# Sums of a pair two back, similarities at the head of a pair, and a different order of the vector work in the experts

## The chip, the cores and the metric

The kernel runs on one core of a Trainium2 chip. The metric is the device time of one execution in microseconds; the kernel before was run three times and took 657.41, 657.68 and 657.73 us (median 657.68). The engines are named as in the profile: PE (TensorE, matmuls), PEld (its weight loads), DVE (VectorE), ACT (ScalarE), POOL (GpSimd) and SP (SyncE, which issues most DMAs). Each engine runs its own instructions strictly in the order of the program, and engines wait for one another by semaphores.

## The reference, cut to what matters

```python
q, k, v: (4, 8, 768, 64)     # batch, head, sequence, head size
centroids: (8, 16, 64);  w_gate: (512, 8);  w1: (8, 512, 1024);  w2: (8, 1024, 512)

q_assign = argmax(normed(q) . normed(centroids));  k_assign likewise
mask = q_assign[:, :, :, None] == k_assign[:, :, None, :]
scores = where(mask, q @ k.T / 8, -1e9)
attn = softmax(scores) @ v                      # (4, 8, 768, 64)
x = attn as rows (3072, 512)                    # heads side by side
logits = x @ w_gate;  e = argmax(logits);  g = softmax(logits)[e]
out = g * (relu(x @ w1[e]) @ w2[e])             # each row by its own expert
```

Attention is masked to keys of the same cluster as the query. Then each of the 3072 rows goes through the one expert that its gate chooses, with no row dropped.

## The kernel before, in words

**Attention.** Two heads of one batch form a pair; there are NPAIR = 16 pairs, HP = 4 to a batch of B = 4. Pair n runs two loops on PE: twelve `score(n, h, j)` (two halves h of the queries, six blocks j of the keys), and then twelve `attend(n, h, j)`. A score is a float32 product of keys and queries (L433 with qT, kT) and a bfloat16 product of two one-hot masks (L433 with mq, mk) that adds a large number for keys of the same cluster and takes one away for others. ACT makes the exponentials of a score (L445, tile A). DVE adds them up over j (`add_up`, L451, tile acc) for the denominators. `attend` multiplies them with v (L457), and ACT copies the result to oT (L464).

Three kinds of work for other pairs are spread among the scores:

- `sum_up(m)` on PE (L480): column sums of acc, and oT times the gate's weights, into one PSUM bank. `weights_of(m)` on DVE turns that bank (L489), makes the reciprocal denominators and adds to the batch's gate logits. `rows(m)` (DVE, L510) transposes oT, and `store(m)` issues four DMAs (L517) to the rows in memory.
- `prepare(m, step)` makes the masks of a later pair. Step 0 transposes queries and keys on DVE (`turn`, L277). Step 1 is `similar` on PE (L291, four products with the centroids). Steps 2 and 3 are the cluster choice on DVE (`assign0`, `assign1`, `assign2`, L302 to L327, ending with the one-hot transpose ohT). Steps 4 and 5 are `place`: eight ACT instructions (L340 for mk, L337 for mq).
- The gating of a batch, after its last pair: `gate`, `gate_exp`, `gate_sum`, `choose` (L546 to L586), `count` (two small PE products, L592 and L593) and `number` (six DVE instructions and six scatters by POOL, L598 to L607). `count` writes to the upper half of the bank that `sum_up` last took (`BANK`).

The order is written out by hand. `at_pair(n, u, f, ...)` hangs a call behind the score of place u = 6h + j of pair n, u = 12 is after the first half's attends, and 13 after the second's. Several calls at one place run in the order in which they were hung. `load(n + 2)` is issued by SP at the head of pair n. PSUM has three double banks for scores (`ps_s`) and two single banks (`ps_m`) that `similar`, `sum_up`, each half's attend output and some counts take in turn; a taker waits until the one two before it is read out. acc has three buffers, oT two, x one, q_in and k_in two each.

**Experts.** Rows are dealt to ten turns s = 0 to 9 of fixed sizes T: two early ones of 288 rows, then 256, 288, 288, 384, 416, 416, 448 and 128. A turn fetches its expert's weights (SP, 2 MB each), gathers its rows (POOL), weighs and rewrites them (`weigh`, DVE L755), takes them back transposed (`take`, SP; `turn_rows`, DVE L780) and runs two layers on PE. Both layers use a Strassen form: seven products of half matrices where eight would be due, with sums of inputs by DVE (`x_sums`, `w1_sums`, `w2_sums`, `h_sums`, all L789) and sums of outputs (L927). A product of `layer1` or `layer2` is a group of eight matmuls (L969, L1070); leftover rows go through L1089 directly. The sums for turn s + 1 are hung into turn s. `at(h1, i, f, ...)` puts a call behind product i of layer 1 (0 to 6 for its first half, 7 to 13 for its second), and `at(h2, i, f, ...)` behind product i of layer 2. In turn 0 layer 2 is written without Strassen, and its places fall behind every second weight block. In layer 2 the addition `z1[:, H:] = c + p7` (L927) stands between places 3 and 4; the seventh product overwrites c's bank and so waits for it. In each half of layer 1 the addition `block(1, 1)` stands in the same way between places 3 and 4, and the last product waits for it.

Of the kernel before, what the change touches and what calls it, by code (L numbers as in the profile page):

```python
# [33 lines left out]
def kernel(  # L34
# [12 lines left out]
    B, H, S, D = q.shape  # L47
# [8 lines left out]
    HP = H // 2  # L56
    NPAIR = B * HP
# [28 lines left out]
    wa = ctx.enter_context(tc.tile_pool(name="weights_a", bufs=1))  # L86
    w1s = ctx.enter_context(tc.tile_pool(name="w1_sums", bufs=1))
    xp = ctx.enter_context(tc.tile_pool(name="rows", bufs=1))
    accp = ctx.enter_context(tc.tile_pool(name="accp", bufs=3))
    otp = ctx.enter_context(tc.tile_pool(name="otp", bufs=2))  # L90
    stat = ctx.enter_context(tc.tile_pool(name="stat", bufs=2))
    rt = ctx.enter_context(tc.tile_pool(name="route", bufs=1))
# [75 lines left out]
    with tc.manual_schedule(), ExitStack() as actx:  # L168
# [12 lines left out]
        def load(n):  # L181
            b, hp = divmod(n, HP)
            for d, src, name in ((QIN, q, "q_in"), (KIN, k, "k_in")):
                t = d[n] = ld.tile([P, NI, Q4], F32, name=name)
                for r in range(4):
                    s = src[b, 2 * hp + r // 2, :, Q4 * (r % 2) : Q4 * (r % 2 + 1)]
                    nc.sync.dma_start(
                        out=t[Q4 * r : Q4 * (r + 1)].rearrange("t (j a) d -> t j a d", a=4),
                        in_=s.rearrange("(a t j) d -> t j a d", a=4, j=NQ),
                    )  # L190
            if n:
                load_v(n)
# [631 lines left out]
        def at_pair(n, u, f, *a):  # L824
            AT.setdefault((n, u), []).append(lambda: f(*a))

        for n in range(NPAIR):
            if n:
                at_pair(n, 2, sum_up, n - 1)
                at_pair(n, 4, rows, n - 1)  # L830
                at_pair(n, 4, store, n - 1)
            for u, step in ((2 if n else 6, 1), (5 if n else 7, 2), (7 if n else 8, 3), (11, 4), (11, 5)):
                at_pair(n, u, prepare, n + 1, step)
        for b in range(B - 1):
            n = HP * (b + 1)
            last = b == B - 2
            at_pair(n, 5 if last else 10, gate, b)
            at_pair(n, 8 if last else 11, gate_exp, b)
            at_pair(n + (not last), 9 if last else 3, gate_sum, b)
            at_pair(n + (not last), 10 if last else 9, choose, b)  # L840
            at_pair(n + 2 - last, 2, count, b)
            at_pair(n + 2 - last, 3 if last else 6, number, b)
        for n in range(1, NPAIR):
            at_pair(n, 2, weights_of, n - 1)
        n = HP * (B - 1)
        slots = range(len(EARLY))
        at_pair(n + 1, 9, rank_first)
# [21 lines left out]
        def between(n, u):  # L869
            for f in AT.pop((n, u), ()):  # L870
                f()
# [4 lines left out]
        for n in range(NPAIR):  # L876
            if n + 2 < NPAIR:
                load(n + 2)
            for h in range(2):
                for j in range(NQ):  # L880
                    score(n, h, j)
                    if j:
                        add_up(n, h, j)
                    between(n, h * NQ + j)
            for h in range(2):
                for j in range(NQ):
                    attend(n, h, j)
                if h == 0:
                    between(n, 12)
                    prepare(n + 2, 0)  # L890
            between(n, 13)
        assert not AT

# [1 line left out]
    with tc.manual_schedule(), ExitStack() as ectx:  # L895
# [262 lines left out]
        n = NPAIR  # L1158
        last = NS - 1
# [9 lines left out]
        for s in range(NS):  # L1169
            h1, h2 = {}, {}  # L1170

            def at(d, i, f, *a):
                d.setdefault(i, []).append(lambda: f(*a))

            if s == 0:
                at(h1, 3, sum_up, n - 1)
                at(h1, 3, weights_of, n - 1)
                at(h1, 4, gate, B - 1)
                at(h1, 4, gate_exp, B - 1)
                at(h1, 5, gate_sum, B - 1)  # L1180
                at(h1, 5, choose, B - 1)
                at(h1, 8, count, B - 1)
                at(h1, 9, number, B - 1)
                at(h1, 11, rows, n - 1)
                at(h1, 11, store, n - 1)
                at(h1, 12, rank_all)
                at(h2, 0, rank_rest)
                at(h2, 3, places, 2)
                at(h2, 3, first_weights, 2)
                at(h2, 5, places, 3)  # L1190
                at(h2, 7, indices, 2)
                at(h2, 7, gather, 2)
            if s == 3:
                at(h1, 12, ask)
                at(h2, 4, answer)
            if s < last:
                if s == 0:
                    first_weights(1)
                elif s > 1:
                    take(s + 1)  # L1200
                if s == 1:
                    at(h1, 6, weigh, 2)
                    at(h1, 7, take, 2)
                    at(h1, 8, second_weights, 2)
                else:
                    second_weights(s + 1)
                if 0 < s <= last - 2:
                    at(h2, 0, first_weights, s + 2)

                if 0 < s <= last - 3:  # L1210
                    at(h2, 1, places, s + 3)

                if s == 0:
                    when = ((h2, 1), (h2, 2), (h2, 5), (h2, 6), (h2, 7), (h2, 7))
                elif s == 1:
                    when = ((h1, 9), (h1, 12), (h2, 2), (h2, 3), (h2, 6), (h2, 6))
                else:
                    when = ((h1, 9), (h1, 10), (h2, 1), (h2, 2), (h2, 2), (h2, 5))
                if GR[s + 1]["T"] >= 2 * P:
                    for (h, i), f, a in zip(when, (w1_sums,) * 4 + (w2_sums,) * 2, (2, 1, 0, 3, 2, 0)):  # L1220
                        at(h, i, f, s + 1, (a,), nc.vector)
                at(h2, 1 if s == 1 else 3, turn_rows, s + 1)
                if GR[s + 1]["T"] >= 2 * P:
                    at(h2, 1 if s == 1 else 4, x_sums, s + 1)
            if s == 0:
                at(h1, 2, gather, 1)
                at(h1, 8, weigh, 1, slice(0, 1))
                at(h1, 11, weigh, 1, slice(1, 2))
                at(h1, 12, weigh, 1, slice(2, 3))
                at(h1, 12, take, 1)  # L1230
            elif s + 2 <= last:
                at(h1, 5 if s == 2 else 4, indices, s + 2)
                at(h1, 5 if s == 2 else 4, gather, s + 2)
                at(h2, 6 if s == 1 else 4, weigh, s + 2)
            if pairs_of(s):
                at(h1, 4, w2_sums, s, (1,), nc.vector)

                at(h1, 5 if s == 1 else 6, w2_sums, s, (3,), nc.vector)
            if s == last - 1:

                at(h1, 4, nc.gpsimd.drain)
            (layer1 if GR[s]["T"] >= 2 * P else few_columns)(s, h1)
            h_sums(s)
            layer2(s, h2)
# [271 lines left out]
```

## Time and the profile before

| | |
|---|---|
| Median of three runs | 657.68 us (657.41 to 657.73) |
| The profiled execution's own time | 657.44 us |
| Its span, first to last instruction | 655.7 us |
| Granted TensorE clock, mean | 0.999 |
| PE busy | 643.5 us (98%), 4252 matmuls |
| DVE busy | 489.5 us (75%) |
| ACT busy | 338.3 us (52%) |
| POOL busy | 133.0 us (20%) |

The attention runs from the start to about 328 us, the experts from there to the end. On a timeline row the columns are start and duration in us, engine, line, operation, what it writes and reads, its array tile or shape, how many instructions are merged in the row, and in brackets the engine's idle time before it and what ended that. A float32 product of the source counts as two matmuls in the profile. The ends of matmuls are modelled, so a busy PE is not PE at its peak.

### The profile page before, as it was taken

The numbers are of one execution on the slowest core, as the hardware profiler recorded it, in microseconds if no ns is written. First come the engines' busy times: TensorE is split into PE (matmuls) and PEld (weight loads), VectorE is DVE, ScalarE is ACT, GpSimd is POOL, SyncE is SP. The second block draws the span as 40 slices with busy tenths as digits, with TensorE's granted clock in tenths as the row PEclk, the third lists the DMA queues.
The fourth block names the chain that finished last, engine by engine and source line by source line (L and its number), as shares of the span: only waits on it lengthen the run. The fifth ranks groups of instructions, "written<-read, shape, count | busy, mean of one in ns | idle before, by whom it ended". The sixth has DMA issues, their size and how long they took to land.

```text
span 655.7 us, 11490 instructions
## 1 busy us (share of the span) xinstructions
PE 643.5 (98%) x4252; PEld 423.0 (65%) x4252; DVE 489.5 (75%) x845; ACT 338.3 (52%) x584; POOL 133.0 (20%) x166
## 2 busy tenths in 40 slices
PE   8999999999999999999999999999999999999995
PEld 4454544445444454444494989989897977869773
DVE  6988878998889988999977987888869365572300
ACT  5677877768778677867532433334241331413210
POOL 5500000022000300033013612324241422140010
PEclk9999999999999999999999999999999999999999
DMA  7753445443455433329476498667694836614010
GB/s 150 162 104 73 79 92 98 74 80 62 79 98 98 74 74 72 74 33 334 110 274 195 152 335 283 232 254 234 241 309 157 281 131 184 229 66 168 8 49 19
DMA packets 189760, 95.38 MB, mean 145 GB/s; under 512 B 152895, under 2 KB 171839, under 8 KB 188416
## 3 DMA queue, kind: packets, MB, share of 16 engines
q1 hardware_dynamic: 184624, 81.56, 45.4%
q0 software_dynamic: 4928, 12.97, 6.0%
q8 instruction: 35, 0.57, 0.4%
q14 instruction: 29, 0.24, 0.1%
q10 hardware_dynamic: 144, 0.03, 0.0%
HBM read 74.10 MB, written 20.70 MB: 145 GB/s over the span
## 4 chain that ended last, share of the span: by engine, by line
PE 94%; DVE 4%; issue 0%; ACT 0%; POOL 0%; POOLq 0%; DVEq 0%; ACTq 0%
PE sps L433 24%; PE mps L457 19%; PE bank L969 12%; PE bank L1089 10%; PE sbank L969 9%; PE bank L1070 7%; PE sbank L1070 6%; PE mps L480 3%; PE mps L291 2%; PE bank L938 1%; DVE xT L780 1%; DVE a L789 1%; DVE v L789 1%; PE sps L356 0%; PE sps L226 0%
## 5 line engine op out<-in xcount | busy, mean ns | idle before, releaser
L445 ACT ACTIVATE A<-sps 128x768 f32<-128x768 f32 x192 | 151.7, 814 | 29.1 <-PE sps L433 28.5
L433 PE MATMUL sps<-qT,kT 64*128 64x384 f32 x768 | 158.9, 492 | 0.0
L451 DVE TENSOR_TENSOR acc<-acc,A 128x768 f32<-128x768 f32 x128 | 121.3, 948 | 10.6 <-ACT A L445 2.4
L457 PE MATMUL mps<-A,v_in 128*64 128x384 f32 x768 | 127.4, 488 | 0.0
L433 PEld LDWEIGHTS sps<-qT,kT 64*128 64x128 f32 x768 | 66.8, 187 | 52.2 <-issue 46.0
L457 PEld LDWEIGHTS mps<-A,v_in 128*64 128x64 f32 x768 | 53.8, 137 | 70.6 <-issue 64.2
L1044 POOL DMA_INDIRECT out_dram<-z,si x30 | 47.1, 1571 | 195.3 <-DVE z L927 165.7
L607 POOL DMA_INDIRECT tokens_of<-tg,pos_i x24 | 28.2, 1176 | 268.5 <-DVE pos_i L605 262.4
L433 PE MATMUL sps<-mq,mk 64*128 64x384 bf16 x384 | 64.6, 323 | 1.6 <-DVE mk L383 1.0
L1089 PE MATMUL bank<-w,h 128*128 128x512 f32 (+2 forms) x224 | 64.4, 596 | 0.0
L340 ACT ACTIVATE mk<-ohT,kscn,ksc 32x384 bf16<-32x384 bf16 x60 | 42.0, 700 | 40.2 <-DVE ohT L327 36.3
L738 POOL DMA_INDIRECT xg<-x_rows,gi x30 | 40.3, 1343 | 45.8 <-DVE si L729 16.5
L969 PE MATMUL sbank<-xc,a 128*128 128x144 f32 (+4 forms) x288 | 47.9, 309 | 0.2 <-ACT sbank L1002 0.2
L969 PE MATMUL bank<-xT,w 128*128 128x144 f32 (+4 forms) x288 | 47.6, 308 | 0.0
L1089 PEld LDWEIGHTS bank<-w,h 128*128 128x128 f32 (+2 forms) x224 | 24.6, 151 | 32.5 <-issue 32.3
L969 PEld LDWEIGHTS bank<-xT,w 128*128 128x128 f32 x288 | 43.8, 190 | 2.3 <-issue 1.9
L451 DVE TENSOR_TENSOR acc<-A 128x768 f32<-128x768 f32 x32 | 30.6, 957 | 18.3 <-ACT A L445 18.2
L969 PEld LDWEIGHTS sbank<-xc,a 128*128 128x128 f32 x288 | 43.3, 190 | 0.7 <-ACT sbank L1002 0.4
L927 DVE TENSOR_TENSOR h<-sbank,p 128x288 f32<-128x288 f32 (+4 forms) x18 | 9.2, 513 | 45.3 <-PE sbank L969 43.9
L987 ACT ACTIVATE h<-h 128x288 f32<-128x288 f32 (+4 forms) x36 | 17.6, 488 | 40.2 <-DVE h L927 38.1
L433 PEld LDWEIGHTS <-mk 64*128 64x128 bf16 x384 | 19.9, 94 | 27.5 <-DVE mk L383 2.6
L755 DVE TENSOR_TENSOR xw<-xg,sf 128x256 f32<-128x256 f32 (+2 forms) x60 | 32.6, 603 | 0.2
(216 smaller groups left out, 898.7 us busy)
## 6 DMA issues: line engine op xcount, KB each, us to landing
w<-in_moe_w_dram SPq DMA_DIRECT2D x20, 2048.0 KB
v_in<-in_v_dram SPq DMA_DIRECT2D x32, 192.0 KB
x_rows<-x SPq DMA_DIRECT2D x64, 96.0 KB
turn_rows<-xw SPq DMA_DIRECT2D x23, 256.0 KB
q_in<-in_q_dram SPq DMA_DIRECT2D x60, 96.0 KB
k_in<-in_k_dram SPq DMA_DIRECT2D x60, 96.0 KB
xs<-turn_rows SPq DMA_DIRECT2D x16, 144.0 KB
xs<-turn_rows SPq DMA_DIRECT2D x8, 208.0 KB
```

Source lines behind the costliest of these rows:

```text
L340: nc.scalar.activation(dst, src, AF.Identity, bias=less, scale=big)
L433: nc.tensor.matmul(SP[n, h, j][:, a, 0:HS], lhsT=kt[rows, j * P : (j + 1) * P], rhs=qt[rows, h * HS : (h + 1) * HS], start=first, stop=not ...
L445: nc.scalar.activation(A[n, h, j], ps[:, :, 0:HS], AF.Exp, scale=D**-0.5)
L451: nc.vector.tensor_tensor(ACC[n, h], first, A[n, h, j], op=ALU.add)
L457: nc.tensor.matmul(O[n, h][D * a : D * (a + 1), 0:HS], lhsT=VIN[n][:, a, j, :], rhs=A[n, h, j][:, a, :], start=(j == 0), stop=(j == NQ - 1),)
L607: ins = nc.gpsimd.indirect_dma_start(out=t_d[:, :], out_offset=bass.IndirectOffsetOnAxis(ap=pos_i[:, i : i + 1], axis=0), in_=tg[:, b, i, ...
L738: nc.gpsimd.indirect_dma_start(out=xg[0:m], out_offset=None, in_=x_d[0:rows_in, :], in_offset=bass.IndirectOffsetOnAxis(ap=g["gi"][0:m, j ...
L755: nc.vector.tensor_tensor(xw[0:m, :, :, d2 * a : d2 * (a + 1)], xg[0:m].rearrange("p (r a d b) -> p a r b d", r=HP, a=2, b=DB)[:, a], g["s ...
L969: nc.tensor.matmul(ps[:, f * T2 : (f + 1) * T2], lhsT=w[:, k, (2 * j + f) * P : (2 * j + f + 1) * P], rhs=x[:, k, :], start=first and f + ...
L1044: ins = nc.gpsimd.indirect_dma_start(out=out[:, :], out_offset=bass.IndirectOffsetOnAxis(ap=GR[s]["si"][0:rows, j : j + 1], axis=0), in_=z ...
L1070: nc.tensor.matmul(ps[:, 0:H], lhsT=x[:, k, :], rhs=y[:, k, :], start=first and k == 0, stop=k == 3, skip_group_check=not first,)
L1089: nc.tensor.matmul(ps[i * m : (i + 1) * m, :], lhsT=h[:, f, j * P : j * P + m], rhs=w[:, f, :], start=(k == 0), stop=(k == FB // n - 1),)
```

## The change

In the attention:

- acc gets a fourth buffer.
- A place -1 is added ahead of a pair's first score.
- In pairs 2 to 7 `sum_up` takes the pair two back and stands at place -1, `weights_of` at 0, `rows` and `store` at 3; `similar` for the next pair stands at place -1 too, its assignment at 2 and 4, and `turn` for the pair after at 9, where it was at 12. Pair 1 has no sums. Pair 8 has those of pair 6 at its head and of pair 7 at place 2. From pair 9 on all is as before.
- The gating of batch 0 moves: `gate` to pair 5 place 10, `gate_exp` to 13, `gate_sum` and `choose` to pair 6 places 3 and 6, `count` and `number` to pair 7 places 1 and 3. Before, these were pair 4 places 10 and 11, pair 5 places 3 and 9, pair 6 places 2 and 6.

In the experts:

- In turn 0 `count` and `number` of the last batch stand one product later (9 and 10).
- In turn 0's layer 2 the four `w1_sums` for turn 1 stand at places 1, 1, 2, 2, where they stood at 1, 2, 5, 6; the two `w2_sums` at 6 and 7, where both stood at 7.
- In turns 2 to 7 the two `w2_sums` in layer 2 stand at places 5 and 6, where they stood at 2 and 5.

```diff
--- before.py
+++ after.py
@@ -86,7 +86,7 @@
     wa = ctx.enter_context(tc.tile_pool(name="weights_a", bufs=1))
     w1s = ctx.enter_context(tc.tile_pool(name="w1_sums", bufs=1))
     xp = ctx.enter_context(tc.tile_pool(name="rows", bufs=1))
-    accp = ctx.enter_context(tc.tile_pool(name="accp", bufs=3))
+    accp = ctx.enter_context(tc.tile_pool(name="accp", bufs=4))
     otp = ctx.enter_context(tc.tile_pool(name="otp", bufs=2))
     stat = ctx.enter_context(tc.tile_pool(name="stat", bufs=2))
     rt = ctx.enter_context(tc.tile_pool(name="route", bufs=1))
@@ -824,24 +824,40 @@
         def at_pair(n, u, f, *a):
             AT.setdefault((n, u), []).append(lambda: f(*a))
 
+        LATE = HP * (B - 2)
+
+        def pair_end(n, u, w, v, m):
+            at_pair(n, u, sum_up, m)
+            at_pair(n, w, weights_of, m)
+            at_pair(n, v, rows, m)
+            at_pair(n, v, store, m)
+
         for n in range(NPAIR):
-            if n:
-                at_pair(n, 2, sum_up, n - 1)
-                at_pair(n, 4, rows, n - 1)
-                at_pair(n, 4, store, n - 1)
-            for u, step in ((2 if n else 6, 1), (5 if n else 7, 2), (7 if n else 8, 3), (11, 4), (11, 5)):
-                at_pair(n, u, prepare, n + 1, step)
+
+
+            if n >= 2 and n <= LATE:
+                pair_end(n, -1, 0, 3 if n < LATE else 0, n - 2)
+            if n >= LATE:
+                pair_end(n, 2, 2, 5 if n == LATE else 4, n - 1)
+            if n == 0:
+                steps = (6, 7, 8, 11, 11, 12)
+            elif n == 1 or n >= LATE:
+                steps = (2, 5, 7, 11, 11, 12)
+            else:
+                steps = (-1, 2, 4, 11, 11, 9)
+            for step, u in enumerate(steps):
+                at_pair(n, u, prepare, n + 1 + (step == 5), (step + 1) % 6)
         for b in range(B - 1):
             n = HP * (b + 1)
             last = b == B - 2
-            at_pair(n, 5 if last else 10, gate, b)
-            at_pair(n, 8 if last else 11, gate_exp, b)
-            at_pair(n + (not last), 9 if last else 3, gate_sum, b)
-            at_pair(n + (not last), 10 if last else 9, choose, b)
-            at_pair(n + 2 - last, 2, count, b)
-            at_pair(n + 2 - last, 3 if last else 6, number, b)
-        for n in range(1, NPAIR):
-            at_pair(n, 2, weights_of, n - 1)
+            if b == 0:
+                when = ((n + 1, 10), (n + 1, 13), (n + 2, 3), (n + 2, 6), (n + 3, 1), (n + 3, 3))
+            elif last:
+                when = ((n, 5), (n, 8), (n, 9), (n, 10), (n + 1, 2), (n + 1, 3))
+            else:
+                when = ((n, 10), (n, 11), (n + 1, 3), (n + 1, 9), (n + 2, 2), (n + 2, 6))
+            for (m, u), f in zip(when, (gate, gate_exp, gate_sum, choose, count, number)):
+                at_pair(m, u, f, b)
         n = HP * (B - 1)
         slots = range(len(EARLY))
         at_pair(n + 1, 9, rank_first)
@@ -876,6 +892,7 @@
         for n in range(NPAIR):
             if n + 2 < NPAIR:
                 load(n + 2)
+            between(n, -1)
             for h in range(2):
                 for j in range(NQ):
                     score(n, h, j)
@@ -887,7 +904,6 @@
                     attend(n, h, j)
                 if h == 0:
                     between(n, 12)
-                    prepare(n + 2, 0)
             between(n, 13)
         assert not AT
 
@@ -1179,8 +1195,8 @@
                 at(h1, 4, gate_exp, B - 1)
                 at(h1, 5, gate_sum, B - 1)
                 at(h1, 5, choose, B - 1)
-                at(h1, 8, count, B - 1)
-                at(h1, 9, number, B - 1)
+                at(h1, 9, count, B - 1)
+                at(h1, 10, number, B - 1)
                 at(h1, 11, rows, n - 1)
                 at(h1, 11, store, n - 1)
                 at(h1, 12, rank_all)
@@ -1211,11 +1227,11 @@
                     at(h2, 1, places, s + 3)
 
                 if s == 0:
-                    when = ((h2, 1), (h2, 2), (h2, 5), (h2, 6), (h2, 7), (h2, 7))
+                    when = ((h2, 1), (h2, 1), (h2, 2), (h2, 2), (h2, 6), (h2, 7))
                 elif s == 1:
                     when = ((h1, 9), (h1, 12), (h2, 2), (h2, 3), (h2, 6), (h2, 6))
                 else:
-                    when = ((h1, 9), (h1, 10), (h2, 1), (h2, 2), (h2, 2), (h2, 5))
+                    when = ((h1, 9), (h1, 10), (h2, 1), (h2, 2), (h2, 5), (h2, 6))
                 if GR[s + 1]["T"] >= 2 * P:
                     for (h, i), f, a in zip(when, (w1_sums,) * 4 + (w2_sums,) * 2, (2, 1, 0, 3, 2, 0)):
                         at(h, i, f, s + 1, (a,), nc.vector)
```

## The prediction

> **What bounds the kernel now.** I read the busy shares first, then the chain that ended last, and then each engine's timeline around the places that the diff touches. First the page: busy time by engine, and the chain by engine.
>
> ```profile
> PE 643.5 (98%) x4252; PEld 423.0 (65%) x4252; DVE 489.5 (75%) x845; ACT 338.3 (52%) x584; POOL 133.0 (20%) x166
> ...
> PE 94%; DVE 4%; issue 0%; ACT 0%; POOL 0%; POOLq 0%; DVEq 0%; ACTq 0%
> ```
>
> PE is busy 643.5 of 655.7 us and is 94% of the chain. Nothing but PE time can be won, and only where PE pauses. The diff adds and removes no matmul, so the question is how many pauses go and how many come. Ends of matmuls are modelled, so I measure pauses from start to start. PE's timeline in pair 3, an ordinary attention pair:
>
> ```profile
> 70.82 0.92 PE L433 MATMUL sps<-qT,kT 64*128 64x384 f32 x4
> ...
> 73.44 0.86 PE L480 MATMUL mps<-acc,ones_s 128*32 128x192 f32 x16
> ...
> 75.20 0.92 PE L433 MATMUL sps<-qT,kT 64*128 64x384 f32 x4
> ...
> 82.67 7.96 PE L457 MATMUL mps<-A,v_in 128*64 128x384 f32 x48
> 90.56 0.92 PE L433 MATMUL sps<-qT,kT 64*128 64x384 f32 x4
> ```
>
> A pair is 19.74 us (70.82 to 90.56): three scores 2.62, sums 1.00, similarities 0.76, nine scores 7.47, attend 7.89. Inside a run of scores one starts each 0.807 us, so 12 need 9.68, and the two runs take 10.09. Each run of scores thus pays 0.20 beyond its scores: about 0.10 in its first one and 0.10 when it is left. No wait stands there; it is the change of the array's tile shape (64*128 against 128*32 and 128*64 in the rows).
>
> PE's timeline in the experts has real waits, and DVE is named:
>
> ```profile
> 337.59 1.14 PE L969 MATMUL bank<-xc,a 128*128 128x144 f32 x8
> 339.33 0.17 PE L592 MATMUL mps<-last,lt_b 128*128 128x8 bf16 x1 [0.59 <-DVE last L586]
> ...
> 365.05 1.14 PE L969 MATMUL bank<-xc,w 128*128 128x144 f32 x8
> 366.71 1.25 PE L969 MATMUL sbank<-xT,a 128*128 128x144 f32 x8 [0.52 <-DVE h L927]
> ...
> 467.19 1.89 PE L1070 MATMUL bank<-v,h 128*128 128x256 f32 x8
> 469.52 1.99 PE L1070 MATMUL sbank<-w,hs 128*128 128x256 f32 x8 [0.44 <-DVE z L927]
> ```
>
> A group of eight at 144 columns takes 0.98 us, at 256 columns 1.73. After a wait the next group is another 0.08 to 0.11 longer. DVE's timeline says why `h` and `z` came late:
>
> ```profile
> 355.81 1.38 DVE L780 STREAM_TRANSPOSE xT<-xs 128x1152 f32<-128x1152 f32 x1 [3.67 <-DMA xs<-turn_rows]
> ...
> 363.93 2.35 DVE L789 TENSOR_TENSOR v<-w 128x1024 f32<-128x1024 f32 x2
> 366.20 0.45 DVE L927 TENSOR_TENSOR h<-sbank,p 128x288 f32<-128x288 f32 x1
> ...
> 466.27 1.21 DVE L789 TENSOR_TENSOR v<-w 128x1024 f32<-128x1024 f32 x1
> 467.40 1.76 DVE L780 STREAM_TRANSPOSE xT<-xs 128x1536 f32<-128x1536 f32 x1
> 469.10 0.37 DVE L927 TENSOR_TENSOR z<-sbank,p 128x256 f32<-128x256 f32 x1
> ```
>
> In both places weight sums for the next expert (`v`, L789) stand in DVE's order ahead of an addition that PE needs to get its bank back. In the first one DVE had meanwhile stood 3.67 us idle for a transfer.
>
> **The experts, part by part.** I number them by the loop variable s, from 0.
> *Count one product later.* L592 starts 1.74 after 337.59 where 0.98 was due (0.76 lost), the two count matmuls take 0.05, the product behind them 0.08 more: 0.89. `last` is there at about 339.3; one product later PE arrives at 339.55 and does not wait. What remains is what the only undisturbed visit of this kind costs (L688 at 439.11: 0.14, and 0.08 behind it): 0.22. Gain 0.67. `number` moves too, with its six DVE instructions and six POOL scatters; DVE is then in the weighing that ends at 340.2, where it was before, so pos_i and the scatters keep their absolute time, and there are 0.3 us left before the next `h` addition.
> *Expert 0, the four w1 sums earlier, w2 sums at places 6 and 7.* In expert 1 L969 loses 0.68 (1.66 for 0.98) plus 0.10: 0.78. The two w1 sums that ran at 361.5 to 363.8 (1.22 each) fit whole into the 3.67 us of idle time before 355.81; their weights were asked for at 327.85, their partner sums ran at 349.7. The w2 sums then run from about 361.5 to 363.9, the indices between them, and the `h` addition finds DVE free 1 us before its bank is done at 365.0. The gather behind those indices is issued about 1 us sooner. Gain 0.78.
> *Later experts, w2 sum 2 from place 2 to 5 and w2 sum 0 from 5 to 6.* One instruction of 1.14 (start to start) leaves the front of the `z` addition. In expert 4 `z` then starts at 467.97, and PE asks for it at 467.19 + 1.73 = 468.92: no wait. Gain 2.33 - 1.73 + 0.11 = 0.71. The same sum: expert 2 (410.38 to 412.40 to 414.23) 0.40, expert 6 (538.89, 541.00, 542.83) 0.48, expert 7 (580.08, 582.32, 584.15) 0.61. Experts 3, 5 and 8 have no such wait. Total 2.20. What is late next: the sums end where they ended before, since DVE's work is the same, and behind them stands the first `h` addition of the next expert. In expert 5 that one now comes 0.71 sooner and had 0.76 of idle time ahead of it (row 478.12): just covered. Expert 3 keeps 0.3 or more, because the 1.95 us that DVE waited for w2 at 409.52 is filled. Experts 7 and 8 have 8 us. If this cover fails, the loss is what that expert gained.
> Experts together: 0.67 + 0.78 + 2.20 = 3.65 us.
>
> **The attention, part by part.**
> *Pairs 2 to 7, sums and similarities at the head.* One run of scores instead of two: 0.20 each, 1.20 for six. Here a rule bears: the Trainium skill, TensorEngine Tiling (Array Packing), Key Properties, says that a change of tiling mode drains TensorE. It speaks against the two visits that are added below as much as for the six removed. It gives no price; TensorE: Matmul & The Clock Gate, Single matmul latency, puts the part of a warm matmul that a drained array can't hide at about 166 ns, so an estimate by the page is 0.33 a run, 2.0 for six. The rows say 0.20, and I take them.
> *Pair 1 loses its sums and pair 8 has two:* 1.00 moves, and the additional visit costs up to 0.10. *The first count alone in pair 7* splits a run of scores: 0.20 + 0.04, less the 0.14 that it costs now: 0.10. Net of these 1.00 saved.
> *New waits at the head.* The sums need the bank of the pair before's first attend output, the similarities that of the second, and both come free by ACT's copies, which stand behind the eight placements, which stand behind DVE's one-hot transpose (ohT). In pair 3:
>
> ```profile
> 73.64 0.96 DVE L451 TENSOR_TENSOR acc<-A 128x768 f32<-128x768 f32 x1 [1.97 <-ACT A L445]
> ...
> 84.99 0.58 DVE L327 STREAM_TRANSPOSE ohT<-oh 128x384 bf16<-128x384 bf16 x1
> ```
>
> ```profile
> 85.61 2.85 ACT L340 ACTIVATE mk<-ohT,kscn,ksc 32x384 bf16<-32x384 bf16 x4 [2.02 <-DVE ohT L327]
> ...
> 90.60 0.86 ACT L464 COPY oT<-mps 128x384 f32<-128x384 f32 x2
> ```
>
> Now ohT ends 14.75 after the head and the copies 0.5 and 0.9 after the next head. That would stall PE. In the new order the first sum starts at 1.76 + 2.82 = 4.6; ahead of ohT stand four sums (3.8), rows (0.9), and the assignment (1.7 and 2.1), while the weights (1.35) run earlier in the 1.97 of idle time: 13.1 to 13.5. Placements (4.95) end at 18.4, the first copy at 18.9, the second right after attend, 19.65 + 0.5. The sums take 1.0, so the similarities find their bank at 20.65. No wait in an ordinary pair, with 0.5 to 0.8 to spare. In pair 7 `number` (1.11) stands ahead of ohT: first copy at about 20.0, so pair 8 waits some 0.3. In pair 6 the gate's sum and choice (0.8 and 1.4) delay the turn of the keys to about 1.05 into pair 7, against 1.1 needed: 0 to 0.1. The similarities in pair 2 wait for the turn in pair 1, where DVE has 2.3 less to do: none.
> *Turns at place 9, rows and stores a pair later.* The eight q and k loads are issued behind the store of the pair before, about 13 to 18 into that pair, the turn comes some 17 into the next: covered by over 15 us. Pair 8 issues two stores of four DMAs; the second `rows` needs the single buffer of the first, stored about 5 us before: covered. The fourth accumulator is memory alone; without it the sums of pair n would wait at the head.
> Attention: -1.00 + 0.3 = 0.7 saved. Ends: if the change of shape is dearer as by the page and nothing waits, 1.6 saved; if each of seven heads waits 0.4, 1.8 lost.
>
> **Sum.** 3.65 + 0.7 = 4.3 us. Span 655.7 - 4.3 = 651.4; the profiled execution took 657.44, so 1.7 lie around the span, and the new one would take 653.1. The median of the runs is 0.24 above it: 653.4.
>
> **Rivals.**
> *Given back at the next expert's first addition.* For: DVE has no idle time from 464.0 to 477.4, and all its work still stands before 478.12. Against: the total is unchanged and 0.76 was free. Price: the gains of experts 2 and 4 (1.1) and the head waits above at 0.2 each (1.4): 655.9. Chance 0.17.
> *Slower: the head becomes ACT's.* Should DVE reach ohT as late as now by its order (14.75 + 1.76 = 16.5), the first copy ends 2.3 into the next pair, and all of pairs 3 to 8 wait for it: 6 x 2.3 - 4.3 = 9.5 us slower, 667. It decides from 4.3 / 6 = 0.7 a head, which is ohT at about 15.0, 1.6 later than I work out. Against: the sums' own 1.97 of idle time takes the weights in. Taking a lag of 2.6, 660. Chance 0.08.
> *The pauses stay.* PE waits for a semaphore that the row does not name rightly, and DVE's order was not the cause: then only the attention's 0.7 remains, 657. For: the brackets are inferred. Against: each late `z` ends just before its PE row (469.10 + 0.37 = 469.47 against 469.52). Chance 0.07.
>
> **How the numbers follow.** My forecast has 0.68. What a measurement of this kernel can tell from no change is 0.2%, 1.3 us. Forecast and the first rival lie beyond it, 0.85 less 0.02 for the first rival's tail: faster 0.83; same 0.09 (the third, and that tail); slower 0.08. The range: below 653.4 by 1.2 (dearer shape changes and no wait, 0.9, and a stray pause of 0.4 at 424.9 whose cause the row does not show); above, it holds the first rival and ends before the third: 652.2 to 656.6.
>
> **What would show it.** Right: no row of L592, L969 or L1070 names DVE at the last product of experts 2, 4, 6 and 7, in the first half of expert 1's first layer, or at the count; `z` starts within 0.8 of xT's end; pairs 3 to 6 take 19.5 each. Wrong: a PE row at a pair's head (L480, L291) that names ACT oT or DVE kT, with pairs above 19.74; or `h` of experts 3 and 5 starting after their bank by more than 0.3.

## The result, and the profile after

The changed kernel takes 655.39 us (median of seven runs, 655.13 to 656.08) where the kernel before took 657.70 beside it: a ratio of 0.9967, 95% interval 0.9955 to 0.9979. It is faster by 2.3 us, or 0.33%. The forecast was 4.3 us less. In a second group of runs it was 655.15 beside 658.22, 3.1 us less, a ratio of 0.9946 (0.9933 to 0.9960).

The profiled execution took 655.66 us with a span of 653.9. Its page, busy time by engine and the chain by engine:

```profile
PE 641.7 (98%) x4252; PEld 423.6 (65%) x4252; DVE 489.7 (75%) x845; ACT 340.3 (52%) x584; POOL 135.4 (21%) x166
...
PE 91%; DVE 4%; ACT 1%; SPq 1%; DMA 1%; issue 1%; POOL 0%; POOLq 0%; DVEq 0%; ACTq 0%
```

The work is the same (4252 matmuls, 845 DVE instructions), and PE still holds the end. Line numbers below 830 are unchanged; L927, L969, L1070 and L1100 have become L943, L985, L1086 and L1116 (and are a few lines off these in some experiments). PE's timeline in pair 3 (columns as explained ahead of the prediction):

```profile
70.36 0.86 PE L480 MATMUL mps<-acc,ones_s 128*32 128x192 f32 x16
...
71.35 0.49 PE L291 MATMUL mps<-qT,cT 128*32 128x384 f32 x2
...
72.11 0.92 PE L433 MATMUL sps<-qT,kT 64*128 64x384 f32 x4
...
82.00 7.96 PE L457 MATMUL mps<-A,v_in 128*64 128x384 f32 x48
89.89 0.86 PE L480 MATMUL mps<-acc,ones_s 128*32 128x192 f32 x16
```

The pair is 19.53 us from head to head (70.36 to 89.89) where it was 19.74: one run of twelve scores in 9.89 instead of two in 10.09. PE's timeline in the experts, at the places shown of before, and one more:

```profile
340.56 1.14 PE L985 MATMUL sbank<-xc,a 128*128 128x144 f32 x8
341.54 0.17 PE L592 MATMUL mps<-last,lt_b 128*128 128x8 bf16 x1
...
366.28 1.14 PE L985 MATMUL bank<-xc,w 128*128 128x144 f32 x8
367.26 1.14 PE L985 MATMUL sbank<-xT,a 128*128 128x144 f32 x8
...
388.41 1.78 PE L1086 MATMUL sbank<-w,hs 128*128 128x256 f32 x7 [0.73 <-DVE z L943]
...
467.33 1.89 PE L1086 MATMUL bank<-v,h 128*128 128x256 f32 x8
469.06 1.89 PE L1086 MATMUL sbank<-w,hs 128*128 128x256 f32 x8
```

Start to start these groups now take 0.98, 0.98 and 1.73: the waits for `last`, for `h` and for `z` in expert 4 are gone. A wait for `z` in expert 1 (388.41) is longer than before. DVE's timeline at the two places shown before:

```profile
356.93 1.38 DVE L780 STREAM_TRANSPOSE xT<-xs 128x1152 f32<-128x1152 f32 x1 [1.23 <-DMA xs<-turn_rows]
...
366.55 0.46 DVE L943 TENSOR_TENSOR h<-sbank,p 128x288 f32<-128x288 f32 x1 [1.41 <-PE sbank L985]
...
466.06 1.76 DVE L780 STREAM_TRANSPOSE xT<-xs 128x1536 f32<-128x1536 f32 x1
467.75 0.37 DVE L943 TENSOR_TENSOR z<-sbank,p 128x256 f32<-128x256 f32 x1
```

The idle time ahead of xT has shrunk from 3.67 to 1.23, since weight sums fill it. `h` now waits for PE instead of PE for `h`, and `z` follows xT at once.

So the places that the prediction named behaved as it said, and yet about half of the gain is missing (over a quarter in the second group of runs). The list of PE's waits in the changed kernel (us in total, times, longest) says where:

```profile
PE mps L592 <- DVE slt L489: 1.8, 2, 1.0
...
PE sbank L1086 <- DVE z L943: 0.7, 1, 0.7
```

The first line has no counterpart before. It is the count of batches 1 and 2, in pairs 10 and 13, where no instruction moves on any engine. PE's timeline in pair 10, from the similarities to the count:

```profile
212.80 0.49 PE L291 MATMUL mps<-qT,cT 128*32 128x384 f32 x2
...
213.14 0.49 PE L291 MATMUL mps<-kT,cT 128*32 128x384 f32 x2
214.50 0.17 PE L592 MATMUL mps<-last,lt_b 128*128 128x8 bf16 x1 [0.87 <-DVE slt L489]
```

DVE's timeline there:

```profile
213.20 0.96 DVE L451 TENSOR_TENSOR acc<-acc,A 128x768 f32<-128x768 f32 x1
214.07 0.38 DVE L489 STREAM_TRANSPOSE slt<-mps 128x192 f32<-128x192 f32 x1
```

In the kernel before, `slt` came just as late in that pair, but the count did not wait for it:

```profile
212.76 0.49 PE L291 MATMUL mps<-qT,cT 128*32 128x384 f32 x2
...
213.09 0.49 PE L291 MATMUL mps<-kT,cT 128*32 128x384 f32 x2
213.52 0.18 PE L592 MATMUL mps<-last,lt_b 128*128 128x8 bf16 x1
...
214.02 0.38 DVE L489 STREAM_TRANSPOSE slt<-mps 128x192 f32<-128x192 f32 x1
```

The count writes the upper columns of the bank that holds the sums, and `slt` reads the lower ones. In the kernel before, `weights_of` was hung into place 2 last of all, behind the count. The changed code hangs it by `pair_end`, right behind `sum_up`, and so ahead of the count. On each engine alone the order is the same; between the two, the read now comes first in the program, so the write must wait for it. DVE reads late, as it did before, behind its additions to acc. From the first similarity to the count 1.70 and 1.78 us pass in the two pairs, where 0.76 passed before: 1.96 in all.

### The profile page after: what moved, and what is told of

It is laid out like the page before. It is cut to its first block, busy times and chain, and to the rows that moved or that the text cites. A ratio compares the mean times of both kernels' runs of the same rounds, so it can differ in the third digit from the quotient of the medians.

```text
span 653.9 us, 11492 instructions
## 1 busy us (share of the span) xinstructions
PE 641.7 (98%) x4252; PEld 423.6 (65%) x4252; DVE 489.7 (75%) x845; ACT 340.3 (52%) x584; POOL 135.4 (21%) x166
## 4 chain that ended last, share of the span: by engine, by line
PE 91%; DVE 4%; ACT 1%; SPq 1%; DMA 1%; issue 1%; POOL 0%; POOLq 0%; DVEq 0%; ACTq 0%
PE sps L433 22%; PE mps L457 17%; PE bank L985 13%; PE bank L1105 10%; PE sbank L985 10%; PE bank L1086 8%; PE sbank L1086 6%; PE mps L480 2%; PE mps L291 1%; DVE acc L451 1%; PE bank L954 1%; SPq L187 1%; DMA q_in<-in_q_dram 1%; ACT A L445 0%; ACT mk L340 0%
## 5 line engine op out<-in xcount | busy, mean ns | idle before, releaser
L1060 POOL DMA_INDIRECT out_dram<-z,si x30 | 51.6, 1719 | 191.9 <-DVE z L943 164.2
L607 POOL DMA_INDIRECT tokens_of<-tg,pos_i x24 | 29.8, 1242 | 271.3 <-DVE pos_i L605 265.2
L985 PE MATMUL sbank<-xc,a 128*128 128x144 f32 (+4 forms) x288 | 47.7, 309 | 0.0
L985 PE MATMUL bank<-xT,w 128*128 128x144 f32 (+4 forms) x288 | 47.7, 309 | 0.0
L738 POOL DMA_INDIRECT xg<-x_rows,gi x30 | 36.7, 1223 | 42.7 <-DVE si L729 14.6
L985 PEld LDWEIGHTS bank<-xT,w 128*128 128x128 f32 x288 | 43.8, 190 | 2.3 <-issue 1.9
L985 PEld LDWEIGHTS sbank<-xc,a 128*128 128x128 f32 x288 | 43.4, 190 | 0.3 <-issue 0.3
L943 DVE TENSOR_TENSOR h<-sbank,p 128x288 f32<-128x288 f32 (+4 forms) x18 | 9.2, 513 | 42.2 <-PE sbank L985 42.2
```

Of the source, the lines that this page charges most:

```text
L607: ins = nc.gpsimd.indirect_dma_start(out=t_d[:, :], out_offset=bass.IndirectOffsetOnAxis(ap=pos_i[:, i : i + 1], axis=0), in_=tg[:, b, i, ...
L738: nc.gpsimd.indirect_dma_start(out=xg[0:m], out_offset=None, in_=x_d[0:rows_in, :], in_offset=bass.IndirectOffsetOnAxis(ap=g["gi"][0:m, j ...
L985: nc.tensor.matmul(ps[:, f * T2 : (f + 1) * T2], lhsT=w[:, k, (2 * j + f) * P : (2 * j + f + 1) * P], rhs=x[:, k, :], start=first and f + ...
L1060: ins = nc.gpsimd.indirect_dma_start(out=out[:, :], out_offset=bass.IndirectOffsetOnAxis(ap=GR[s]["si"][0:rows, j : j + 1], axis=0), in_=z ...
```

## The experiments

Ratios are to the kernel before, run beside each on the same chip (medians 657.99, 658.22 and 658.70 in the three groups). Pair lengths are from head to head on PE's timeline.

### The weights behind the count again

```diff
         def pair_end(n, u, w, v, m):
             at_pair(n, u, sum_up, m)
-            at_pair(n, w, weights_of, m)
+            if n < LATE or w != 2:
+                at_pair(n, w, weights_of, m)
...
+        for n in range(LATE, NPAIR):
+            at_pair(n, 2, weights_of, n - 1)
```

The edit holds for pairs 8 to 15; pair 8 has no count.

> The changed kernel with one thing taken back: in pairs 9 to 15 the weights of the pair before stand last at place 2 again, behind the similarities and the count, as in the kernel before. The order of instructions on every engine stays that of the changed kernel; only which write to the double-used bank waits for which read changes. Theory A (the two counts in pairs 10 and 13 wait for the weights' reading of their bank, 0.95 us each): L592 names DVE no more in the attention, pairs 10 and 13 take 19.8 to 19.9 where they took 20.80 and 20.89, and the median falls by 1.9 from 655.4 to 653.5. Theory B (those two pairs are longer since DVE is behind, and the wait is only where it shows): the pause moves to another row of the same pairs, and the median stays at 655.4, within 0.4.

Measured: 653.52 (653.04 to 653.86), ratio 0.9928 (0.9915 to 0.9941). Pairs 10 and 13 take 19.88 each, where the changed kernel has 20.80 and 20.89. PE's timeline in pair 10:

```profile
213.52 0.49 PE L291 MATMUL mps<-kT,cT 128*32 128x384 f32 x2
213.95 0.18 PE L592 MATMUL mps<-last,lt_b 128*128 128x8 bf16 x1
```

No bracket, and 0.43 between the two rows where the changed kernel has 1.36. DVE reads `slt` at 214.45 here too, so it is as late as ever; what changed is who must wait for whom. Theory A holds, and so does its size: 655.39 less 653.52 is 1.87, though across two groups of runs. A second measurement of this version, as the base of the last group, was to show

> The version with the weights of pairs 9 to 15 behind the count once more, as the base of the three below on one chip: ratio to the kernel before 0.993, about 653.5.

and showed 653.53 (653.12 to 653.70), ratio 0.9917 (0.9902 to 0.9933); that is 1.62 below the changed kernel's second median, 655.15.

### The same edit in the kernel before

```diff
             if n:
                 at_pair(n, 2, sum_up, n - 1)
+                at_pair(n, 2, weights_of, n - 1)
...
-        for n in range(1, NPAIR):
-            at_pair(n, 2, weights_of, n - 1)
```

> The kernel before with one edit: at place 2 of each pair the weights are hung right behind the sums, ahead of the similarities and the count. By the theory that a count then has to wait for the weights' reading of the bank they share, the three counts in pairs 6, 10 and 13 wait 0.95 each: 2.85 more, 660.8 where the kernel before takes 658.0. By the rival (in the changed kernel the counts wait since DVE is late there for another reason) nothing changes: 658.0.

Measured: 661.18 (660.51 to 661.49), ratio 1.0035 (1.0021 to 1.0048): 2.96 above the kernel before beside it. The list of PE's waits:

```profile
PE mps L592 <- DVE slt L489: 2.7, 3, 1.0
```

Three counts, 2.7 us of waits. With nothing else of the change present, the place of one line costs about as much as the whole change gains (2.3 and 3.1). The rival (DVE late for another reason) is out.

### Attention alone and experts alone

The first kernel has the changed attention and the old experts, the second the reverse.

> The attention of the changed kernel with the experts of the kernel before. The prediction's sum says 0.7 saved in the attention: 657.0. Theory A (the attention saves 1.0 as the prices in it say, and loses 1.9 at two counts): the attention as a whole loses, 658.5, that is 0.9 above the kernel before. Theory B (the attention also lost 1.0 at its start, in pair 0, in a way that the change causes): 659.5.

> The attention of the kernel before with the experts of the changed kernel. The prediction's sum says 3.65 saved: 654.05. By the profile of the changed kernel, in which the experts took 3.78 less: 653.9. If the longer pause in expert 1's second layer (0.57 more than before) comes from the earlier weight sums in the experts alone, it stands here too; if it comes from the attention's later state (rows of the last batch, loads), it is gone here and the time is 653.4.

Measured: experts alone 653.96 (653.40 to 654.64), ratio 0.9938 (0.9926 to 0.9951), that is 4.0 less, where the prediction's sum had 3.65. Attention alone 660.56 (658.97 to 663.12), ratio 1.0043 (1.0026 to 1.0060), that is 2.6 more, where the prediction had 0.7 less and theory A 0.9 more. Together the halves come to 1.4 less, where the whole change has 2.3 and 3.1 less: they do not simply add, since what the old experts take is not fixed. From pair 1's head to pair 15's the changed attention takes 278.92 and the old one 277.30, 1.6 more. The rest stands in the old experts (PE's timeline there is 1.5 longer than before), by the list of PE's waits in the attention-alone kernel:

```profile
PE sbank L1086 <- DVE z L943: 1.9, 5, 0.7
...
PE sbank L985 <- DVE h L943: 0.9, 1, 0.9
```

In the kernel before these were 1.2 and 0.5. The program there is the same; what differs is when transfers land. DVE's timeline of the attention-alone kernel, at the weight sum in expert 2's second layer,

```profile
412.08 1.23 DVE L789 TENSOR_TENSOR v<-w 128x1024 f32<-128x1024 f32 x1 [2.50 <-DMA w<-in_moe_w_dram]
```

and that of the kernel before:

```profile
409.52 1.23 DVE L789 TENSOR_TENSOR v<-w 128x1024 f32<-128x1024 f32 x1 [1.95 <-DMA w<-in_moe_w_dram]
```

The weights came 0.55 later against DVE's own work, and because this sum stands ahead of the addition that PE waits for, the 0.55 goes straight to PE: the group of eight matmuls ahead of that wait is 0.85 longer than due, where it was 0.30. Most of it is the transfer itself: from its issue by SP to this row it took 11.13, where it took 10.72 before. In expert 1 DVE waited 4.03 for the rows where it waited 3.67 before, and the group ahead of `h` is 0.35 longer. So the old order passes a late transfer on. Another 0.54 stands in the pause that the prediction saw at 424.9. Whether the changed attention brings the late landings about, or they are chances of the execution, is not shown. From PE's first to its last start in the experts, three profiles of the old order show 320.78, 322.03 and 322.29; eleven of the new one (with variants in expert 1 and of the attention) show 316.54 to 317.24. What the change saves in the experts is thus between 3.5 and 5.8, depending on the execution of the old order that it is set against.

### The fourth w1 sum behind the addition in expert 1

The first edit is that of the first experiment. The second:

```diff
                 elif s == 1:
-                    when = ((h1, 9), (h1, 12), (h2, 2), (h2, 3), (h2, 6), (h2, 6))
+                    when = ((h1, 9), (h1, 12), (h2, 2), (h2, 5), (h2, 6), (h2, 6))
```

> The changed kernel with the weights of pairs 9 to 15 behind the count again, and in turn 1 the fourth w1 sum for turn 2 from place 3 of layer 2 to place 5, so that it stands behind the addition z that the seventh product waits for. Theory A: 1.9 less by the first edit; in expert 1 the wait for z (0.73 and 0.17 around it) falls away, 0.9 less by the second: 652.6. If DVE is simply late there for its transfer of xs, whatever the order behind it, the addition gains only part of that: 653.2. If the sum moved behind is itself late for expert 2's first layer, a pause of up to 1.2 comes back in the first half of expert 2: 653.8.

Measured: 653.58 (652.86 to 653.62), ratio 0.9926 (0.9913 to 0.9939): no gain over 653.52. The wait for `z` is gone, and PE's timeline in the first half of expert 2 has a new one:

```profile
393.08 1.16 PE L988 MATMUL sbank<-xT,a 128*128 128x128 f32 x8 [0.36 <-DVE h L946]
```

The group ahead of it takes 1.41 where 0.89 is due: 0.52. The third case was the right one: DVE has no idle time here, and what is moved past one addition lands in front of the next. It also shows that there was less to win than the expectation took: in the first experiment's profile the `z` wait costs 0.33, not the 0.90 of the changed kernel's first profile. That 0.90 came with rows that landed late (DVE waited 0.49 for xs at 382.79, where the kernel before did not wait).

### The changed kernel once more

> The changed kernel itself once more, beside the versions below on one chip: 655.4. In its first profile pair 0 had four scores at half speed and expert 1's second layer waited 0.73 for z. If both are chances of that one execution, they are gone here, and the profile shows what the first one hid: at the head of pair 2 a sum that waits some 0.36 for ACT's copy. If the change brings them about, they stand here again.

Measured: 655.15 (654.66 to 655.98), ratio 0.9946 (0.9933 to 0.9960). Both disturbances of the first profile were chances: pair 0 ran at full clock, and the wait for `z` in expert 1 is 0.2. And what they hid is there. PE's timeline at the head of pair 2:

```profile
51.27 0.86 PE L480 MATMUL mps<-acc,ones_s 128*32 128x192 f32 x16 [0.66 <-ACT oT L464]
```

ACT's timeline ahead of it:

```profile
45.77 2.84 ACT L340 ACTIVATE mk<-ohT,kscn,ksc 32x384 bf16<-32x384 bf16 x4 [2.19 <-DVE ohT L327]
48.62 2.10 ACT L337 COPY mq<-ohT 32x384 bf16<-32x384 bf16 x4
50.74 0.86 ACT L464 COPY oT<-mps 128x384 f32<-128x384 f32 x2
```

The sums need the bank of pair 1's first output, which ACT copies at 50.74 behind its eight placements. It is the rival "the head becomes ACT's", at one head.

### The assignment at places 5 and 7

On the base of the first experiment:

```diff
             else:
-                steps = (-1, 2, 4, 11, 11, 9)
+                steps = (-1, 5, 7, 11, 11, 9)
```

> The version with the weights behind the count, and in pairs 2 to 7 the assignment at places 5 and 7 as in the kernel before, where the change has 2 and 4; sums and similarities stay at the head. It tries the margin at the head: by the prediction the earlier assignment is what lets ACT's placements and the first copy of the attend output be done in time. In pair 1, which has places 5 and 7, ohT ended 13.5 after the head; with scores 0.8 to 1.0 later and rows ahead of it: 14.5. Placements 4.95 and the copy 0.48 end at 19.9 to 20.0, the head comes at 19.54: each of pairs 2 to 7 is 0.4 to 0.5 longer (19.95 to 20.05), 2.4 to 3.0 in all, 656.2. By the rival named slower in the prediction (ohT at 16.5) pairs take 21.9 and the time is 667. If ACT isn't near the limit at all, pairs stay at 19.54 and the time at 653.5.

Measured: 663.08 (662.90 to 663.63), ratio 1.0068 (1.0053 to 1.0083): 9.6 above its base. Pairs 2 to 5 take 20.58 and pairs 6 and 7 take 22.73 and 23.41. PE's timeline at the heads of pairs 4 and 7:

```profile
91.48 0.86 PE L480 MATMUL mps<-acc,ones_s 128*32 128x192 f32 x16 [0.96 <-ACT oT L464]
...
155.37 1.44 PE L480 MATMUL mps<-acc,ones_s 128*32 128x192 f32 x16 [3.13 <-ACT oT L464]
```

DVE's timeline in pair 3:

```profile
85.39 0.58 DVE L327 STREAM_TRANSPOSE ohT<-oh 128x384 bf16<-128x384 bf16 x1
```

ohT ends 15.06 after the head (70.91), placements and copy take 5.5 more, and the pair becomes 20.57: the head is exactly ACT's. With places 2 and 4 ohT ends 12.93 after the head (83.67 against 70.74 in the base's profile). The expectation of 14.5 was 0.6 short, and it left out pair 6's choice and pair 7's numbering, which put ohT at 17.2 and 17.9. By the pair lengths the lag is 4 x 1.04 + 3.19 + 3.33 = 10.7, by the medians 9.6; the rival had 6 x 2.3 = 13.8. It put the turning point at 0.7 a head, with ohT at 15.0; shown is 1.04 at 15.06, and a kernel that is 4.9 slower than before. What keeps it away in the changed kernel is that the assignment was moved together with the sums.

### Pair 1: similarities at the head, or the assignment sooner

Both on the base of the first experiment:

```diff
-            elif n == 1 or n >= LATE:
+            elif n >= LATE:
                 steps = (2, 5, 7, 11, 11, 12)
```

> The version with the weights behind the count, and pair 1 too with similarities at the head, the assignment at places 2 and 4 and the turn at 9. Theory: pair 2's sums waited 0.36 since pair 1 lost its 1.0 of sums but not the time to ohT; with the earlier assignment ohT ends about 1.5 sooner, the wait goes, and one run of scores goes as well (0.20): 0.56 less, 653.0 where the version without it takes 653.5. If instead the similarities at pair 1's head wait for the turn of the keys at the end of pair 0, the gain is lost: 653.5 or up to 654.

Measured: 653.98 (653.77 to 654.61), ratio 0.9929 (0.9916 to 0.9943); no gain. Pair 1 takes 18.56, 0.57 less, and pair 2's head waits no more, but PE's timeline at the head of pair 1 shows the price:

```profile
34.02 0.52 PE L291 MATMUL mps<-qT,cT 128*32 128x384 f32 x2 [1.81 <-ACT oT L464]
```

The place was foreseen, the engine was not: the keys were turned at 33.64, and ACT's copy was the later one. Instead, the assignment one place sooner:

```diff
-            elif n == 1 or n >= LATE:
+            elif n == 1:
+                steps = (2, 4, 6, 11, 11, 12)
+            elif n >= LATE:
                 steps = (2, 5, 7, 11, 11, 12)
```

> That base, and in pair 1 the assignment at places 4 and 6 where it is at 5 and 7 (similarities stay at place 2). Theory: pair 2's first sum waits for ACT's copy because ohT of pair 1 ends 13.5 after the head; one place sooner is 0.8 sooner, ACT's placements and copy with it, and the wait of 0.36 (0.74 in one execution) at pair 2's head goes: 0.4 less than the base, 653.1. If the assignment can't start sooner (the similarities are read at place 4 as soon as they are done, and DVE's sums stand ahead), the wait stays and so does the time: 653.5.

Measured: 653.09 (652.63 to 653.42), ratio 0.9910 (0.9895 to 0.9925), beside the base's 653.53. The medians differ by 0.44, as expected, but the intervals overlap. Its own profile has pair 0 at half clock, which hides the wait as in the first profile of the changed kernel. The next two versions carry the same edit and ran at full clock: pair 1 takes 18.76 and 18.77 for 19.13, and no row at pair 2's head names ACT.

### Carried on to pairs 8 to 11, and the ranking later

On top of that, LATE is HP * (B - 1), and batches 0 and 1 share the late gating:

```diff
-        LATE = HP * (B - 2)
+        LATE = HP * (B - 1)
...
-            if b == 0:
+            if b < 2:
                 when = ((n + 1, 10), (n + 1, 13), (n + 2, 3), (n + 2, 6), (n + 3, 1), (n + 3, 3))
```

> The version before this one, and the change's order (sums of the pair two back and similarities at the head) carried on to pairs 8 to 11, with batch 1 gated as late as batch 0; pair 12 has two sums, the last four pairs are as before. By the prices seen in pairs 2 to 8: 0.20 for each of pairs 8 to 11 less; what pair 8 pays for two sums moves to pair 12; the count of batch 1 stands alone in a pair (0.34 where it costs 0.14). 0.6 less: 652.5. If later heads wait for ACT as pair 7's successor does for DVE, 0 to 0.5 is left of it: 653.1.

Measured: 652.37 (652.17 to 652.55), ratio 0.9900 (0.9885 to 0.9915). Pairs 8 to 10 take 19.54, pair 11 takes 20.07 and pair 12 takes 20.86; pairs 8 to 12 are 0.41 shorter in all, where 0.6 was expected. It is the best version of this study, 3.0 below the changed kernel by the medians of two groups of runs. On top of that:

```diff
-        at_pair(n + 1, 9, rank_first)
+        at_pair(n + 1, 13, rank_first)
...
-        at_pair(n + 1, 11, first_turns)
+        at_pair(n + 1, 13, first_turns)
...
-            at_pair(n + 2, 2, indices, s)
+            at_pair(n + 2, 5, indices, s)
```

> The version before this one, and the ranking of the experts, the first turns' indices and their weights moved from places 9 and 11 of pair 13 to its end, and the row indices from place 2 to 5 of pair 14. In the profiles of the changed kernel the similarities in pair 14 wait up to 0.53 for the turn of pair 15's keys, which stands behind these on DVE. Theory: that wait goes, 0.2 to 0.5 less, 652.2. If the first weights or rows then come late for the first turn of the experts, a wait appears at 329 to 340 and the time is 653 or more.

Measured: 652.97 (652.11 to 653.34), ratio 0.9908 (0.9892 to 0.9924). The wait in pair 14 went (19.74 for 20.27), yet the time did not fall. By the two profiles the experts are 0.46 longer (317.24 against 316.78, PE's first to last start): 0.13 in the first half of expert 2's first layer, where the version before also loses 0.20, 0.26 in the second half, and 0.08 at the last sums. These waits were expected elsewhere, and what brings them about was not traced further.

## Why the prediction was half right

**Direction and mechanism held, the sum did not.** Part by part, forecast against profile, in us saved. The attention's rows compare pair lengths of the first experiment with those of the old attention in the experts-alone kernel (19.75 in pair 1, 19.88 in pair 6); pairs 10 and 13 are the changed kernel's own:

| Part | Forecast | Shown |
|---|---|---|
| Experts | 3.65 | 3.7 and 4.1 in two profiles of the changed kernel |
| Pairs 2 to 7, run of scores, count and turn in pair 7 | 1.1 | 0.8 |
| Pair 1, without sums | 1.0 | 0.6 |
| Pair 8, two sums, and its wait | -1.4 | -1.1 |
| Pairs 10 and 13 | 0 | -1.9 |
| Sum | 4.3 | 2.1 to 2.5; measured 2.3 and 3.1 in two groups of runs |

The sum leaves out pair 0, which takes 29.82 to 30.69 in profiles with one and the same order at full clock. That the result lies within the stated range is in part luck: the upper end of the range was drawn for the first rival (655.9), and a loss of that size came from a place that no rival named.

**The step that failed is the one that was left out.** The prediction's attention sum goes through pairs 1 to 8 and ends there; the text before it says "From pair 9 on all is as before". The diff hangs `weights_of` in those pairs at the same place 2, but ahead of the similarities and the count instead of behind. Costed by the prediction's own method that edit moves no instruction on any engine. Its cost is a dependency between engines through a shared bank, 0.95 us at each of two counts. The first two experiments show it in both directions, with the price.

That a wait stands there at all, though count and `slt` use different columns, fits the Trainium skill, PSUM — Partial Sum Buffer, "PSUM bank collisions raise a hardware error": two engines must not touch one bank in the same partitions at once, disjoint columns included. No run here lets them collide; the runs show what keeping them apart costs when the program names the slow reader first.

**Experts.** The count's loss, the first half of expert 1 and the four `z` waits went, each at its place. Two things were not in the sum. The pause at 424.9, which the prediction called stray, went as well (0.38 before; 0.92 and 0.93 in the other two profiles of the old order; in none of the new order). Its cause stays open: it does not follow the late `z` of expert 2, which cost 0.30, 0.85 and 0.22 in these three profiles. And the sizes of the old waits vary with the landing of transfers. Rival one (given back at the next first addition) happened only in small: the 0.76 of cover in expert 5, which the prediction called just enough, held in eight of the eleven profiles of the new order, and in the other three, the changed kernel's second among them, the first `h` of expert 5 costs 0.18 to 0.24. Expert 3 has no such wait. It did happen where the fourth experiment pushed one sum further.

**The run of scores.** Pairs 2 to 5 are 0.20 shorter, four times over, as the rows before had said. The prediction's estimate from the latency figure of the Trainium skill (TensorE: Matmul & The Clock Gate, Single matmul latency), 0.33 a run, would have made them 19.41; the measurement decides for the row.

**The head.** The chain of ohT, placements and copy was worked out well for an ordinary pair (13.1 to 13.5 forecast, 12.9 shown), and pair 8 does not wait, where 0.3 was forecast: ohT of pair 7 ends 14.3 after the head, the first copy 5.5 later, and pair 7 itself takes 20.08. But the prediction applied this chain to pairs 2 to 8 only. In pair 1 it looked at the turn of the keys alone, while the pair lost 1.0 of PE work and its assignment stayed at places 5 and 7. So pair 2's head waits for ACT's copy, 0.36 in most profiles: rival two in small, shown by the version with places 4 and 6.

**The turn in pair 7** waits 0.2 (0 to 0.1 was forecast), and the count alone there costs 0.3, not 0.1, over an ordinary pair.

## What to carry to other kernels

When a diff rearranges calls that are issued to several engines, compare the order of every pair of instructions that share a bank or buffer, not only the order on each engine: a producer hung behind a slow reader costs a wait though no engine's own sequence changed. When work is taken out of one step of a pipeline, check the next resource in that step as well; the pair that lost PE work is the one where ACT became late. Put work that waits for a transfer behind the instruction that the bottleneck needs, which also makes the time less dependent on when transfers land.

## What the runs showed of the hardware that was not expected

**The clock after a pause.** With the assignment at places 5 and 7, PE waits 3.13 us at pair 7's head. That kernel's rows by window (us, busy time by engine, then the granted PE clock, DMA share and GB/s):

```profile
155.30:157.00 1.70, 1.63 (x24) 1.15 (x28) 0.11 (x1) 0.40 (x2) 0.00 (x0) 0.56 0.05 10
157.00:159.50 2.50, 2.50 (x20) 0.82 (x14) 1.30 (x5) 0.00 (x0) 0.00 (x0) 0.62 0.00 0
159.50:162.00 2.50, 2.50 (x22) 1.37 (x20) 0.40 (x1) 1.72 (x3) 0.00 (x0) 1.00 0.00 0
```

A granted clock of 0.56 over 1.70 us and 0.62 over 2.50 is half clock for 1.5 + 1.9 = 3.4 us, an estimate that takes half and full clock as the only two. If the pause brings it about, it costs about 1.7 us of PE more than its own length. This is one profile; the pauses of 1.0 and 1.8 us elsewhere brought no such fall. The first profile of the changed kernel has one in pair 0, behind several short waits:

```profile
15.00:18.00 3.00, 3.00 (x12) 1.97 (x13) 2.90 (x4) 1.62 (x2) 2.61 (x9) 0.50 0.06 8
```

With 0.79 in the microsecond before, that is 3.4 us again. Two of the fourteen profiles have it there, with the same program up to that point. The Trainium skill, TensorE: Matmul & The Clock Gate, Part 1, says that the clock is halved after an idle window of about 3.4 us that runs freely, so that its phase is a matter of chance. The length of the slow stretch and its coming in one execution and not in another agree with that; the waits ahead of it in pair 0 are each far shorter than such a window (1.4 us is the longest in the list of PE's waits), so no run here explains what sets it off. In pair 0 no cost of it can be told from chance: pair 2's head comes at 50.82 in the changed kernel's first profile, and between 50.33 and 51.27 in six profiles with the same order up to there and full clock.
